# Turned scores from a second product instead of turned probabilities, division once per unit, and attention written in one hand order

## The chip, the cores and the metric

The kernel runs on one core of a Trainium2 chip. The metric is the device time of one execution in microseconds (us). "PE" is the matmul engine, with its weight loads shown apart as "PEld"; DVE, ACT and POOL are the vector, scalar and GpSimd engines; SP issues most of the DMAs.

## The reference

Input x has S = 2048 tokens of D = 1024; there are H = 32 heads of width 32, N = 4 segments of L = 512 tokens, and a channel MLP with F = 3584. All is float32.

```python
def _A_ref(x, wq, wk, wv, wo, beta):            # x is layernormed
    q, k, v = (x @ wq, x @ wk, x @ wv)          # split to [B, H, N, L, Dh]
    g = sigmoid(beta)
    for s in range(N):
        logits = einsum("bhqd,bhkd->bhqk", qs, ks) * Dh ** -0.5 + causal_mask
        a_dot = einsum("bhqk,bhkd->bhqd", softmax(logits), vs)
        pq = phi(qs)                            # phi(t) = t + 1 if t > 0 else exp(t)
        a_mem = einsum("bhld,bhde->bhle", pq, M) / (einsum("bhld,bhd->bhl", pq, z) + 1e-6)
        outs.append(g * a_mem + (1 - g) * a_dot)
        M = M + einsum("bhld,bhle->bhde", phi(ks), vs);  z = z + phi(ks).sum(l)
    return concat(outs) @ wo

h = x + _A_ref(layernorm(x), ...)
return h + gelu(layernorm(layernorm(h)) @ w1 + b1) @ w2 + b2
```

## The kernel before, in words

**Precision.** Every operand of a product is kept as two numbers of a shorter format, a high half (`hi`, names ending in h) and the rest (`lo`, names ending in l), and a product is three matmuls (`mm3`, lines L116 to L118): high by high, high by low, low by high. A high half is a cast on ACT or DVE, a low half a subtraction on DVE or POOL.

**Stages.** The tokens are processed in two halves of 1024, each half two segments. Per half: layernorm and turning of the tokens to [channels, tokens] (`ln1`), attention, the output projection (`wo_first`, `wo_second`), the second layernorms, and the MLP by a scheme of seven products (lines from L840 on). A unit of attention is one column group g (of 8, four heads of 32 each) and one segment: `dense` projects k, q and v in 24 steps of three 512-wide matmuls (tiles `kps`, `qps`, `vps`), and between those steps `heads` runs the four heads of the unit before.

**One head before.** `stack` copies high and low halves of q and k by DMA into 96-row tiles `qs` and `ks`, so that a single 96-row product is the sum of the three. `qk` (L543, L544) multiplies for each block i of 128 queries the queries (stationary) by all keys up to the diagonal, widths 128 to 512, into `pqk` (two banks); DVE adds the mask, scales by -1/sqrt(32), writes `pr` to SBUF and keeps the row's minimum in `mx`. `soft` (L552) takes the exponential on ACT with the row sums as a by-product. `ptr` (L593, L595) turns the ten 128x128 blocks of probabilities on PE, by a product with the identity, into `ppt` (two banks), ACT casts them to `pth`; `sub` (L600) gives the low half `ptl` on DVE. `av` (L613) multiplies by `vs`, which holds the high and low halves of v as 64 stationary columns, into the single bank `po`; ACT copies the lower 32 rows to `ot` (L618) and DVE adds the upper ones (L624). `inverse` and `weigh` make the reciprocals of the sums of a unit, bring them from a row per query to a column per query over `r_dram`, and multiply on POOL.

**Order before.** The order on each engine in the attention comes from the scheduler of the programming layer, out of the order in which the code records its instructions: generators are interleaved by ratios (`interleave`, RA, RH, RS), and the table `PLAN` says which operation of which head stands in each of the six steps of a slot. Only the opening and the MLP stand in `in_order`, which ties every instruction to the one recorded before it on its engine.

**Memory of the segments.** `smalls` interleaves small matmuls that read the memory (`pm`) and update it (`pmm`) between the others; `pkn`, `vn` and `pom` are turnings of 128x128 blocks. They all, the projections and `pwo` share three banks (tag "d").

## Time and profile before

| | |
|---|---|
| median of 3 runs | 2315.74 us (2314.35 to 2320.98) |
| span of the profiled execution | 2309.1 us |
| PE busy | 2273.1 us, 98% |
| PE weight loads | 1895.7 us, 82% |
| DVE busy | 1519.7 us, 66% |
| ACT busy | 1227.7 us, 53% |
| POOL busy | 830.6 us, 36% |
| instructions | 34959 |

The profiled execution's time outside its span is not recorded; the median of the runs lies 6.6 us above that span. Busy is the union of the instructions' durations; a matmul's duration contains its way through the array, which overlaps the next one, so the pace of PE is read from the starts in the timeline. In a row of groups, the two numbers after the count are the total busy time in us and the mean of one in ns, and behind the second bar stands the idle time of the engine just before these instructions and what ended it. Attention lies at about 38 to 555 us and 895 to 1435 us of the span.

### The profile page before, as it was taken

How to read it: one execution, taken by the hardware profiler on the slowest of the kernel's cores; microseconds unless marked ns; L12 is line 12 of the kernel's file. 1: busy time of each engine (PE TensorE's matmuls, PEld its weight loads, DVE VectorE, ACT ScalarE, POOL GpSimd, SP SyncE). 2: the span in 40 equal slices, each digit the busy share in tenths (PEclk: the TensorE clock that was granted, in tenths of full speed). 3: DMA queues.
4: the chain of work that ended last, by engine and by line, in shares of the span. 5: the costliest groups of instructions: out<-in, count | busy, mean ns of one | idle time of the engine just before them, and what ended most of it. 6: DMA issues, size and time to landing. Idle time of an engine off the chain costs nothing.

```text
span 2309.1 us, 34959 instructions
## 1 busy us (share of the span) xinstructions
PE 2273.1 (98%) x11801; PEld 1895.7 (82%) x11801; DVE 1519.7 (66%) x3045; ACT 1227.7 (53%) x2581; POOL 830.6 (36%) x686
## 2 busy tenths in 40 slices
PE   8999999999999999999999998999999999999999
PEld 6888888877888887888888886788888888888887
DVE  6777777776655565777777776574566766566663
ACT  6777777774453445777777775363344223332221
POOL 4222222224244442233232224244445654155430
PEclk9999999999999999999999999999999999999999
DMA  6333343344466654433333343466567976476772
GB/s 187 104 95 97 98 102 95 94 140 164 138 209 173 186 166 138 120 100 95 95 95 99 95 118 119 160 202 195 156 190 265 348 249 217 152 259 218 249 235 92
DMA packets 329885, 364.00 MB, mean 158 GB/s; under 512 B 28750, under 2 KB 221802, under 8 KB 329706
## 3 DMA queue, kind: packets, MB, share of 16 engines
q1 hardware_dynamic: 266538, 325.06, 46.5%
q10 hardware_dynamic: 63168, 36.71, 5.3%
q8 instruction: 93, 1.52, 0.3%
q14 instruction: 86, 0.70, 0.1%
HBM read 234.98 MB, written 76.35 MB: 135 GB/s over the span
## 4 chain that ended last, share of the span: by engine, by line
PE 69%; DMA 1%; POOL 1%; ACT 1%; DVE 1%; issue 1%; SPq 0%; POOLq 0%; ACTq 0%; DVEq 0%
PE po L1300 23%; PE bps L904 10%; PE cps L904 7%; PE dps L904 6%; PE po L613 3%; PE ppt L593 3%; PE pqk L543 2%; PE vps L116 1%; PE vps L117 1%; PE vps L118 1%; PE kps L116 1%; PE kps L117 1%; PE qps L117 1%; PE qps L116 1%; PE kps L118 1%; PE qps L118 1%
## 5 line engine op out<-in xcount | busy, mean ns | idle before, releaser
L552 ACT ACTIVATE pr<-pr,mx 128x256 f32<-128x256 f32 (+3 forms) x512 | 287.1, 561 | 163.5 <-DVE mx L544 154.7
L544 DVE CUSTOM_DVE_ANT_0 pr<-pqk,mask 128x256 f32<-128x256 f32 (+3 forms) x512 | 244.5, 486 | 107.1 <-PE pqk L543 105.9
L600 DVE TENSOR_TENSOR ptl<-ppt,pth 128x512 fp32r<-128x512 f32 (+1 forms) x384 | 227.3, 600 | 94.9 <-ACT pth L595 92.4
L593 PE MATMUL ppt<-ident,pr 128*128 128x128 f32 x1280 | 223.1, 277 | 1.0 <-DVE ptl L600 0.8
L595 ACT CAST pth<-ppt 128x512 fp32r<-128x512 f32 (+1 forms) x384 | 194.0, 517 | 40.2 <-PE ppt L593 33.1
L93 POOL TENSOR_TENSOR wl<-wr,wh 128x1024 fp32r<-128x1024 f32 x52 | 124.8, 2399 | 229.5 <-PE pqk L543 128.0
L1310 DVE TENSOR_TENSOR c<-c,po 128x512 f32<-128x512 f32 x160 | 105.4, 683 | 149.6 <-PE po L1300 146.7
L593 PEld LDWEIGHTS ppt<-ident,pr 128*128 128x128 f32 x1280 | 165.0, 141 | 30.8 <-DVE ptl L600 1.9
L543 PE MATMUL pqk<-ks,qs 96*128 96x256 f32 (+3 forms) x512 | 161.6, 316 | 0.0
L613 PE MATMUL po<-ptl,vs 128*64 128x512 f32 (+3 forms) x512 | 154.1, 310 | 4.3 <-DVE ptl L600 4.1
L613 PE MATMUL po<-pth,vs 128*64 128x512 f32 (+3 forms) x512 | 156.0, 327 | 0.0
L1300 PE MATMUL po<-w2h,zh 128*128 128x512 f32 x378 | 120.8, 389 | 0.0
L543 PEld LDWEIGHTS pqk<-ks,qs 96*128 96x128 f32 x512 | 96.5, 189 | 21.6 <-issue 0.2
L904 PE MATMUL bps<-zh,sb 128*128 128x512 f32 x336 | 111.1, 391 | 0.0
L904 PE MATMUL bps<-zh,sa 128*128 128x512 f32 x336 | 110.8, 390 | 0.0
L1157 POOL TENSOR_TENSOR w2r<-w2r 128x512 f32<-128x512 f32 x54 | 85.5, 1595 | 70.2 <-DMA w2r<-in_B_w 63.6
L116 PE MATMUL vps<-yh,wh 128*128 128x512 f32 x256 | 109.4, 427 | 0.9 <-DVE MZ L500 0.9
L116 PE MATMUL kps<-yh,wh 128*128 128x512 f32 (+1 forms) x264 | 110.0, 417 | 0.0
L116 PE MATMUL qps<-yh,wh 128*128 128x512 f32 x256 | 106.9, 418 | 0.0
L1300 PE MATMUL po<-w2h,hl 128*128 128x512 f32 x322 | 103.0, 390 | 0.0
L117 PE MATMUL kps<-yl,wh 128*128 128x512 f32 (+1 forms) x264 | 102.3, 388 | 0.1
L118 PE MATMUL kps<-yh,wl 128*128 128x512 f32 (+1 forms) x264 | 101.9, 386 | 0.0
(253 smaller groups left out, 6548.4 us busy)
## 6 DMA issues: line engine op xcount, KB each, us to landing
hr<-h_dram SPq DMA_DIRECT2D x112, 448.0 KB, 5.7
w2r<-in_B_w SPq DMA_DIRECT2D x122, 256.0 KB, 4.1
r<-in_B_w SPq DMA_DIRECT2D x56, 512.0 KB, 4.8
h_dram<-ht ACTq DMA_DIRECT2D x84, 256.0 KB, 3.8
ks<-kh SPq DMA_DIRECT2D x256, 64.0 KB, 2.0
qs<-qh SPq DMA_DIRECT2D x256, 64.0 KB, 2.0
wr<-in_A_wo SPq DMA_DIRECT2D x32, 512.0 KB, 4.5
wx<-in_B_w SPq DMA_DIRECT2D x56, 256.0 KB, 3.6
```

The lines of the kernel that those rows point to most:

```text
L116: nc.tensor.matmul(ps, ah, bh, start=first, stop=False)
L117: nc.tensor.matmul(ps, ah, bl, start=False, stop=False)
L118: acts["mm"] = nc.tensor.matmul(ps, al, bh, start=False, stop=last)
L543: nc.tensor.matmul(pqk[:, :n], u["qs"][j][:, i * P:(i + 1) * P], u["ks"][j][:, 0:n], start=True, stop=True)
L544: nc.vector.tensor_tensor_reduce(out=st["pr"][:, offs[i]:offs[i] + n], in0=pqk[:, :n], in1=mask[:, 512 - n:512], op0=ALU.add, op1=ALU.min, ...
L552: nc.scalar.activation(pi, pi, AF.Exp, bias=mx[:, i:i + 1], scale=-1.0, accum_out=mx[:, 4 + i:5 + i])
L593: nc.tensor.transpose(ppt[:, o:o + P], pr[:, offs[i] + jk * P:offs[i] + (jk + 1) * P], ident)
L595: acts["pth"] = n, nc.scalar.copy(pth[:, base:base + w], ppt[:, :w])
L600: nc.vector.tensor_tensor(o, x0, x1, op=ALU.subtract)
L613: nc.tensor.matmul(po[:, P * jk:], v, st[part][:, koff[jk]:koff[jk] + w], start=(jk, part) == (0, "pth"), stop=(jk, part) == (2, "ptl"))
L904: nc.tensor.matmul(ps, x_[:, c, :], y_[:, c, :], start=first and c == 0 and n == 0, stop=last and c == 3 and n == 2, skip_group_check=True)
L1300: nc.tensor.matmul(ps, x_[:, k], y_[k], start=opens and k == 0 and i == 0, stop=closes and k == self.KP - 1 and i == 2, skip_group_check=True)
```

## The change: what it does

The probabilities are no longer turned. `qk1` makes the score product as before, but for the maximum alone: DVE writes its result back over the bank. When a unit's four heads are through, `halves` splits the maxima (negative) into two halves, `turn` brings them with four 8-column products from queries in partitions to queries in columns (`ptn`), and `rows` copies them as eight more rows (96 to 103) into `qs`; the same rows of `ks` hold a pattern of ones that picks the two rows of a head. `qk2` then makes a second product with the keys stationary, 104 rows deep: its output `pst` is the turned score less the maximum. ACT takes the exponential into `e` (three groups of 512, 384 and 256 + 128 columns), POOL zeroes the upper triangle of the diagonal blocks with an affine select, ACT casts to `ph` (`cast`), DVE makes `pl` (`lows`). `vs` gets two columns of ones, so that the row 64 of `po` is the sum of the probabilities; ACT copies it to `sm`. Division comes once per unit (`weigh`): two DVE transposes of 32x32 blocks around one reciprocal and the gate, then multiplications on POOL by quarters. The trip over `r_dram` goes.

The units come in another order (`ORDER`): column groups 0 and 1 alternate in the first four units of a half and 6 and 7 in the last four, so weights are loaded and split in 12 sets per half where it was 8. Weights' high halves are made on DVE, the low halves on POOL in quarters. Attention and the first output projection stand in `in_order` on all engines, and every operation that isn't a dense matmul has a step by hand (`at`); a slot is six steps, one head passes `qk1` in slots h + 3 and h + 4, `qk2` in h + 8 and `av` in h + 9. The output weights of the first block are made within the last units, and the second projection takes over the weights that the first used last.

```diff
-PLAN = ('q1 r S2', 'q0 a0', 'q2 t0 w a1', 'q3 s0 o', 't1', 's1 t2')
+ORDER = [(g + n % 2, n // 2) for g in (0,) for n in range(4)] + [(n // 2, n % 2) for n in range(4, 12)] + \
+    [(6 + n % 2, n // 2) for n in range(4)]
+KX = 104
+QK = {4: 3, 5: 2, 1: 1, 2: 0}
+AVS = {2: (0,), 4: (1,), 5: (3, 2)}
+VC = 66
...
-            pqk = psum.tile([P, 512], F32, tag="qk", name="pqk", bufs=2)
-            nc.tensor.matmul(pqk[:, :n], u["qs"][j][:, i * P:(i + 1) * P], u["ks"][j][:, 0:n], start=True, stop=True)
-            nc.vector.tensor_tensor_reduce(
-                out=st["pr"][:, offs[i]:offs[i] + n], in0=pqk[:, :n], in1=mask[:, 512 - n:512],
-                op0=ALU.add, op1=ALU.min, scale=-SCALE, scalar=3.0e38, accum_out=st["mx"][:, i:i + 1])
-            soft(st, i)
...
+            ps = psum.tile([P, 512], F32, tag="qk", name="pqk", bufs=2)
+            nc.tensor.matmul(ps[:, :n], u["qs"][0:96, j, i * P:(i + 1) * P], u["ks"][0:96, j, 0:n], start=True, stop=True)
+            nc.vector.tensor_tensor_reduce(out=ps[:, :n], in0=ps[:, :n], in1=mask[:, 512 - n:512], op0=ALU.add,
+                                           op1=ALU.min, scale=-1.0, scalar=3.0e38, accum_out=u["mx"][:, i, j:j + 1])
+        def halves(u):
+            u["mh"] = mh = ab.tile([P, 4, 8], F32R, name="mh", bufs=2)
+            m3 = mh.rearrange("p i (j x) -> p i j x", x=2)
+            nc.vector.tensor_copy(m3[:, :, :, 0], u["mx"][:, :, 0:4])
+            nc.vector.tensor_tensor(m3[:, :, :, 1], u["mx"][:, :, 0:4], raw(m3[:, :, :, 0]), op=ALU.subtract)
+        def turn(u):
+            ps = u["pt"] = psum.tile([P, 512], F32, tag="pt", name="ptn", bufs=2)
+            for i in range(4):
+                nc.tensor.matmul(ps[0:8, i * P:(i + 1) * P], u["mh"][:, i, :], acts["identr"], start=True, stop=True)
+        def rows(u, j):
+            nc.scalar.copy(u["qs"][96:KX, j, :], u["pt"][0:8, :])
+        def qk2(h, n):
...
+            ps = psum.tile([P, 512], F32, tag="pt", name="pst", bufs=2)
...
+                nc.tensor.matmul(ps[:, o:o + 512 - P * jk], u["ks"][:, j, jk * P:(jk + 1) * P], u["qs"][:, j, jk * P:512],
+                                 start=True, stop=True)
+            e = e[:, :w]
+            nc.scalar.activation(e, ps[:, :w], AF.Exp, scale=SCALE)
...
+            nc.gpsimd.affine_select(d, d, pattern=[[0, 2], [1, P]] if n == 2 else [[1, P]], compare_op=ALU.is_ge,
+                                    fill=0.0, base=0, channel_multiplier=-1)
+        def cast(h, n):
+            e, ph, _ = H4[h][n]
+            nc.scalar.copy(ph, e)
+        def lows(h, n):
+            e, ph, pl = H4[h][n]
+            nc.vector.tensor_tensor(pl, e, raw(ph), op=ALU.subtract)
...
-                    nc.tensor.transpose(ppt[:, o:o + P], pr[:, offs[i] + jk * P:offs[i] + (jk + 1) * P], ident)
-            acts["pth"] = n, nc.scalar.copy(pth[:, base:base + w], ppt[:, :w])
...
+        def out(h):
+            nc.scalar.copy(u["ot"][b, :], po[32:64, :])
+            nc.scalar.copy(u["sm"][32 * j:32 * j + 1, :], po[64:65, :])
+        def weigh(u, k):
+            if k == 0:
+                nc.vector.transpose(smt, sm)
+            elif k == 1:
+                nc.vector.reciprocal(u["inv"], smt.rearrange("p (a b) -> p a b", b=32)[:, :, 0])
+                nc.gpsimd.tensor_scalar(u["inv"], u["inv"], gcol[:, u["g"]:u["g"] + 1], None, op0=ALU.mult)
+            elif k == 2:
+                nc.vector.transpose(sm.rearrange("p (a b) -> p a b", b=32),
+                                    u["inv"].unsqueeze(2).to_broadcast([P, 16, 32]))
...
+        def slot_step(t, c):
+            h1, h2, h3 = t - 4 + c // 4, t - 8, t - 9
...
+            if c in QK and ok(h1):
+                qk1(h1, QK[c])
+                if QK[c] == 0 and h1 % 4 == 3:
+                    u = U[h1 // 4]
+                    at(b + 4, partial(halves, u))
+                    at(b + 6, partial(turn, u))
+                    for j in range(4):
+                        at(b + 7 + j, partial(rows, u, j))
+            if c > 2 and ok(h2):
+                qk2(h2, c - 3)
+                at(b + c + 2, partial(cast, h2, c - 3))
+                at(b + c + 3 + (c == 5), partial(lows, h2, c - 3))
+            if c in AVS and ok(h3):
+                av(h3, AVS[c])
+                if c == 5:
+                    out(h3)
+                    at(b + 6, partial(added, h3))
...
+        order = ExitStack()
+        order.enter_context(in_order())
         rest = attention(half, first)
...
+        interleave(wo_first(half, hts), rest, RA, RH, RS)
+        order.close()
```

784 lines of the change are left out of this document (426 added, 358 removed).

## The prediction

> **What bounds the kernel now.** I read the busy shares first, then the windows of the attention stage, then its matmuls in order of time, and last the groups of the engines beside TensorE.
>
> ```profile
> PE 2273.1 (98%) x11801; PEld 1895.7 (82%) x11801; DVE 1519.7 (66%) x3045; ACT 1227.7 (53%) x2581; POOL 830.6 (36%) x686
> ```
>
> TensorE is busy for 98% of the span, but that is an average; the change touches the attention of both halves alone, so its stages decide. "Head" below is one head of one segment (128 in all, 64 per half); a unit is four heads of one column group.
>
> ```profile
> core 0 of [0], span 2309.1 us
> core 0: us, PE busy (x) PEld busy (x) DVE busy (x) ACT busy (x) POOL busy (x), PEclk, DMA share, GB/s
> 100.00:480.00 380.00, 379.32 (x2327) 322.33 (x2326) 276.65 (x785) 277.52 (x715) 97.05 (x103) 1.00 0.37 95
> 945.00:1340.00 395.00, 395.00 (x2427) 336.07 (x2426) 291.82 (x842) 292.92 (x751) 116.12 (x116) 1.00 0.37 96
> 500.00:560.00 60.00, 54.09 (x293) 43.95 (x292) 41.94 (x89) 37.51 (x81) 19.88 (x15) 0.97 0.40 137
> 1380.00:1450.00 70.00, 62.45 (x321) 50.29 (x320) 45.20 (x95) 38.30 (x80) 26.86 (x21) 0.98 0.43 141
> ```
>
> The two long windows are the steady part of each half: PE has no idle time in the second, while DVE has 26%, ACT 26% and POOL 71%. The clock is full. The two short windows are the ends of attention, where PE lost 5.9 us of 60 and 7.6 us of 70. So in the steady part PE sets the pace and whatever leaves it shortens the span, until the next engine takes over. The pace of one head follows from the score products:
>
> ```profile
> 945.00:1340.00 395.00, 64.35 (x205) 38.52 (x205) 97.44 (x205) 1.00 0.37 96
> ```
>
> There are four weight loads of `pqk` per head (PEld, x205), so 51.25 heads in 395 us: 7.71 us per head. DVE works 0.739 x 7.71 = 5.70 us of that (291.82 of 395 us), ACT 5.72 us.
>
> **The change part by part.** *The turning transposes go, a second score product comes.* A matmul's duration (0.39 us for 512 columns) overlaps the next, so PE work is priced from start to start:
>
> ```profile
> 303.42 0.39 PE L543 MATMUL pqk<-ks,qs 96*128 96x512 f32 x1
> 303.65 0.40 PE L116 MATMUL vps<-yh,wh 128*128 128x512 f32 x1
> 303.89 0.40 PE L117 MATMUL vps<-yl,wh 128*128 128x512 f32 x1
> 304.12 0.39 PE L118 MATMUL vps<-yh,wl 128*128 128x512 f32 x1
> 304.35 0.60 PE L593 MATMUL ppt<-ident,pr 128*128 128x128 f32 x4
> 304.71 0.48 PE L116 MATMUL vps<-yh,wh 128*128 128x512 f32 x1
> 305.03 0.40 PE L117 MATMUL vps<-yl,wh 128*128 128x512 f32 x1
> ...
> 305.93 0.38 PE L593 MATMUL ppt<-ident,pr 128*128 128x128 f32 x2
> 306.07 0.48 PE L116 MATMUL vps<-yh,wh 128*128 128x512 f32 x1
> 306.38 0.40 PE L117 MATMUL vps<-yl,wh 128*128 128x512 f32 x1
> 306.62 0.40 PE L118 MATMUL vps<-yh,wl 128*128 128x512 f32 x1
> 306.85 0.28 PE L543 MATMUL pqk<-ks,qs 96*128 96x256 f32 x1
> 306.97 0.39 PE L116 MATMUL vps<-yh,wh 128*128 128x512 f32 x1
> ```
>
> Four `ppt` transposes hold the next matmul back by 0.36 us (304.35 to 304.71), and the matmul behind them takes 0.32 us where such a one takes 0.23 (303.42 to 303.65): 0.45 us together. Two cost 0.14 + (0.31 - 0.23) = 0.22 us (305.93 to 306.38). A head has groups of 4, 4 and 2: 0.45 + 0.45 + 0.22 = 1.12 us. The second product `pst` has the widths of `pqk`: 512 columns take 0.23 us, 256 take 0.12 (306.85 to 306.97), 384 and 128 by their widths 0.17 and 0.06: 0.58 us. It contracts 104 rows where `pqk` contracts 96; `vps` with 128 rows and `pqk` with 96 both take 0.23 us for 512 columns, so I take the same. The weighted sums keep their widths and get 66 stationary columns where there were 64: nothing. Per unit four 128-column turns of the maxima come (4 x 0.06 = 0.24 us) and one `pw` transpose goes (about 0.16 us by the rows of two). Sum on PE: 128 x (0.58 - 1.12) + 32 x (0.24 - 0.16) = -69.1 + 2.6 = **-66.5 us**, which leaves 7.71 - 0.52 = 7.19 us per head. The PE order, in the middle of a projection's unit, before and after:
>
> ```order
> L116 MATMUL vps<-yh_9229,wh 128x512
> L117 MATMUL vps<-yl_9230,wh 128x512
> L118 MATMUL vps<-yh_9229,wl 128x512
> L543 MATMUL pqk<-ks,qs 128x384
> L593 MATMUL ppt<-ident,pr 128x128 x4
> L613 MATMUL po<-pth,vs 64x128
> L613 MATMUL po<-ptl,vs 64x128
> L613 MATMUL po<-pth,vs 64x256
> L613 MATMUL po<-ptl,vs 64x256
> ```
>
> ```order
> L124 MATMUL vps<-yh_10288,wh 128x512
> L125 MATMUL vps<-yl_10289,wh 128x512
> L126 MATMUL vps<-yh_10288,wl 128x512
> L595 MATMUL pqk<-ks_10244,qs_10246 128x384
> L624 MATMUL pst<-qs_10246,ks_10244 128x256
> L624 MATMUL pst<-qs_10246,ks_10244 128x128
> L654 MATMUL po<-ph,vs_10252 66x128
> L654 MATMUL po<-pl,vs_10252 66x128
> L654 MATMUL po<-ph,vs_10252 66x256
> L654 MATMUL po<-pl,vs_10252 66x256
> ```
>
> The transposes' place is taken by the second product; the rest of the step stands as it stood.
>
> The Trainium skill ("TensorE: Matmul & The Clock Gate", Part 4) puts a 128x128 transpose at about 275 ns inside a kernel; as a price for each of the 1280 that would be an estimated 352 us, and a time some 209 us below mine. The trace has the same figure as a duration (0.60 us for four that overlap), but four of them advance PE by 0.36 us, so the sum goes by the start times.
>
> *ACT stays level.*
>
> ```profile
> L552 ACT ACTIVATE pr<-pr,mx 128x256 f32<-128x256 f32 (+3 forms) x512 | 287.1, 561 | 163.5 <-DVE mx L544 154.7
> ```
>
> ```profile
> L595 ACT CAST pth<-ppt 128x512 fp32r<-128x512 f32 (+1 forms) x384 | 194.0, 517 | 40.2 <-PE ppt L593 33.1
> ```
>
> ```profile
> 306.37 0.59 ACT L458 CAST pkh<-pkn 128x512 fp32r<-128x512 f32 x1
> 306.85 0.61 ACT L366 ACTIVATE e<-qps 128x512 f32<-128x512 f32 x1
> 307.34 0.61 ACT L367 ACTIVATE r<-qps 128x512 f32<-128x512 f32 x1
> 307.81 0.39 ACT L595 CAST pth<-ppt 128x256 fp32r<-128x256 f32 x1
> 308.23 0.51 ACT L552 ACTIVATE pr<-pr,mx 128x256 f32<-128x256 f32 x1
> 308.64 0.19 ACT L552 ACTIVATION_READ_ACCUMULATOR pr<-pr,mx 128x1 f32 x1
> 308.77 0.62 ACT L448 CAST pqh<-pq 128x512 fp32r<-128x512 f32 x1
> ```
>
> Gone: 287.1 + 194.0 + 512 reads of 0.19 = 97, together 578 us. New, per head: three exponentials out of PSUM (512, 384, 384 columns; 0.59 + 0.49 + 0.49, between the 0.59 and 0.39 of the casts out of PSUM at 306.37 and 307.81), three casts from SBUF (0.62 + 0.52 + 0.52, by `pqh`), one more copy of the sums (0.59) and one of four turned rows (0.59): 4.41 us x 128 = 564 us. No loss, no gain: PE hides it.
>
> *DVE gets fuller.*
>
> ```profile
> L600 DVE TENSOR_TENSOR ptl<-ppt,pth x384: 393/692/694, 49.8 to 1431.9; 128x512 fp32r<-128x512 f32 x128, 128x256 fp32r<-128x256 f32 x64
> ```
>
> ```profile
> L90 DVE CAST wh<-wr 128x1024 fp32r<-128x1024 f32 x43 | 29.4, 684 | 0.2
> ```
>
> ```profile
> L559 DVE RECIPROCAL rs<-mx 128x4 f32<-128x4 f32 x128 | 22.4, 175 | 30.4 <-ACT pr L552 30.2
> ```
>
> The maximum keeps its four instructions, now written back to PSUM (same price taken; no row shows it). The low halves keep 1280 elements per head, so 1.8 us at 692 ns per 512. Per head a reciprocal goes (0.18). Per unit come two small splits of the maxima (0.17 each), a reciprocal and two 32x32 transposes of 128x512 (no row; 0.69 each like any 512-wide pass, bounds 0.3 and 1.4). Because the first and last four units alternate column groups, 24 weight sets are split where 16 were, and all on DVE: 80 casts for 44, 36 x 0.684 / 32 = 0.77 us per unit. Together 2.67 / 4 - 0.18 = +0.5: 6.2 us per head of 7.19.
>
> *POOL* is new in the path, zeroing the diagonal blocks between ACT's exponential and ACT's cast:
>
> ```profile
> L93 POOL TENSOR_TENSOR wl<-wr,wh 128x1024 fp32r<-128x1024 f32 x52 | 124.8, 2399 | 229.5 <-PE pqk L543 128.0 <-DVE wh L90 46.8 <-ACT wh L92 25.3
> ```
>
> ```profile
> L337 POOL TENSOR_SCALAR_AFFINE_SELECT mask<-mask 128x128 f32<-128x128 f32 x2 | 0.6, 297 | 0.1
> ```
>
> Two selects of 128 and one of 256 columns: 0.30 + 0.30 + 0.4 = 1.0 us per head; weight lows (2.4 us x 3 x 24 sets) 1.35, weighing and `pql` (0.6 us per 256 columns by the same row) about 0.9, smaller ones some 0.4: some 3.7 us of 7.19. It fits, and two steps of slack stand between each select and its cast.
>
> *Waits of the hand order.* All engines now run strictly as written. Two loops are short. First, the turned maxima sit in one of two `pt` banks until ACT has copied four rows, the last behind an exponential, and the next score product waits for that bank. ACT, in the middle of a half, in a plain step before and at the unit's turn now (`ph` casts the probabilities `e`, `qs<-ptn` is a copied row):
>
> ```order
> L595 CAST pth<-ppt 128x512
> L552 ACTIVATE pr,mx<-pr,mx 128x384
> L618 COPY ot<-po 32x512
> L552 ACTIVATE pr,mx<-pr,mx 128x512
> L595 CAST pth<-ppt 128x512
> ```
>
> ```order
> L637 CAST ph<-e 128x384
> L611 CAST qs_181<-ptn 8x512 x2
> L627 ACTIVATE e<-pst 128x512
> L611 CAST qs_181<-ptn 8x512
> L627 ACTIVATE e<-pst 128x384
> ```
>
> The exponentials now read `pst`, and the last row copy stands between two of them. Long ACT instructions in a row start 0.48 us apart (306.37, 306.85, 307.34 above). From the start of the first `pst`: 0.39 for the matmul, 0.48 and 0.58 on ACT, some 0.1 for signals = 1.55; PE itself needs 0.23 + 3 x 0.23 + 0.23 = 1.15 before it wants the bank. Wait 0.4 us per unit: +13 us (0 if ACT's queue is short, 0.4 per head = 51 at worst). Second, the weighted sums have one bank, `po`. Behind its last matmul lie an exponential, ACT's copy and DVE's add: 0.3 + 0.48 + 0.58 + 0.68 = 2.0; PE has nine projection matmuls and two small ones until it wants the bank, 9 x 0.23 + 0.12 + 0.06 = 2.25. DVE, around the add of one head's sums (`ot`, now `side`), before and now:
>
> ```order
> L544 ISA pr,mx<-pqk,mask 128x512
> L544 ISA mx 128x1
> L624 TENSOR_TENSOR ot<-po,ot 32x512
> L431 TENSOR_TENSOR ql<-qps,qh 128x512
> L559 RECIPROCAL rs<-mx 128x4
> ```
>
> ```order
> L596 ISA pqk,mx<-pqk,mask 128x384
> L596 ISA mx 128x1
> L382 SCALAR_TENSOR_TENSOR pq<-e,r 128x512
> L641 TENSOR_TENSOR pl<-e,ph 128x512
> L670 TENSOR_TENSOR side<-po,side 32x512
> ```
>
> The add stood right behind a maximum; a low half is now always ahead of it, and in some slots one more pass of 0.69 us, which eats the 0.25 of slack. I take 0.1 us per head on average: +13 us (bounds 0 and 0.4).
>
> *Ends.* The output weights of the first projection are now split inside the order, and the second reuses what the first left, so these waits should go:
>
> ```profile
> PE pwo L117 <- POOL zl L93: 3.1, 1, 3.1
> ```
>
> ```profile
> PE pwo L117 <- POOL zl L93: 4.7, 1, 4.7
> ```
>
> -8 us (bounds 0 and -12). Against it the second unit now needs a new weight set within 10 dense steps of 0.7 us, 7 us for a load, a cast and four lows: +5 us (0 to 10).
>
> Sum: 2309.1 - 66.5 + 13 + 13 - 8 + 5 = 2265.6 us of span; the median of the runs lies 6.6 us above this span (2315.74 - 2309.1), so **2272 us**. With no new wait and the ends at their best it is 2309.1 - 66.5 - 12 + 6.6 = 2237; with the waits nearly doubled 2295.
>
> **The rivals.** *The short loops eat the gain.* PE waits 0.4 us in every head, not 0.2. With no gain at the ends that is 2309.1 - 66.5 + 51 + 5 + 6.6 = 2305 us. For it: strict order, one `po` bank. Against: the loops' slack is positive in plain slots.
>
> *DVE becomes the bound (slower).* The low halves used to read PSUM and SBUF; now both inputs, `e` and `ph`, lie in SBUF, while POOL works half the time. A row of the later stage shows what that does:
>
> ```profile
> L1032 DVE TENSOR_TENSOR sa<-s,sa 128x512 fp32r<-128x512 f32 x56 | 52.5, 974 | 32.4 <-ACT sa L1031 32.4
> ```
>
> `sa`, whose two inputs lie in SBUF while POOL adds, has a mean of 974 ns; `ptl`, of the same width with one input in PSUM, never exceeds 694. At that mean each low half costs 0.28 more: 6.2 + 3 x 0.28 = 7.05 us of DVE per head. If strict order leaves DVE idle for 12% of its time, a head takes 7.9 us, +0.2 over now: 2315.7 + 26 = 2342. It decides once DVE's work and waits pass 7.71 us. Against: the new POOL instructions are 0.3 to 0.65 us long where those of the later stage are whole tiles of 512 columns, 1.2 us by the same 2.4 per 1024, so each hold is shorter. The Trainium skill ("SBUF — State Buffer", Who interferes with whom) says that a VectorE instruction with two SBUF inputs contends with a GpSimd one that reads SBUF; by that rule, with which `sa` and `ptl` agree, this rival is the one to fear.
>
> *The transposes were not on the path*, so nothing moves: 2316. Against it stands the PE window with no idle time.
>
> **How the numbers follow.** My forecast has 0.57 (its own range 2237 to 2295), the loops 0.18, DVE 0.21, no effect 0.04. About 0.3% (7 us) is what a measurement of this kernel can tell. The forecast is all faster; of the loops' 0.18 about 0.12 lie below 2309; of the last two about 0.01 do. Faster 0.70 (0.57 + 0.12 + 0.01). Same 0.08: 0.04 of the loops and no effect. Slower 0.22: 0.02 of the loops, 0.20 of DVE. The range runs from 2237 to 2338: it holds the forecast, the loops, no effect and the better half of the DVE case.
>
> **What would show it.** Right: PE rows of `pst` at the pace of `pqk`; about 7.4 us per head; short PE waits at `pst` for ACT and at `po` for DVE; `pl` with a mean under 800 ns; DVE below 90% in the steady windows. Wrong: `pl` means near 1 us with PE waiting on DVE throughout (the DVE rival), PE waits above 0.4 us in each head (the loops), or a pace still at 7.7 with PE full.

## The result: slower by 1.7%, and the profile after

The changed kernel takes 2355.3 us (median of 4 runs, 2353.1 to 2359.9) against 2316.2 before (2314.4 to 2321.0): ratio 1.0174, 95% interval 1.0153 to 1.0194. The forecast was 2272, with a range up to 2338, so the result lies outside it on the slow side. The profiled execution has a span of 2352.8 us, 43.7 more than before.

The busy times of the page, and the groups that answer to the rows of the prediction (behind the second bar stands the idle time just before a group and what ended it):

```profile
PE 2255.7 (96%) x11129; PEld 1849.4 (79%) x11129; DVE 1605.5 (68%) x3094; ACT 1238.6 (53%) x2153; POOL 1150.4 (49%) x1445
L641 DVE TENSOR_TENSOR pl<-e,ph 128x384 fp32r<-128x384 f32 (+1 forms) x384 | 262.5, 685 | 28.9 <-ACT ph L637 26.9
L654 PE MATMUL po<-ph,vs 128*66 128x512 f32 (+3 forms) x512 | 150.2, 319 | 46.5 <-DVE side L670 46.5
L624 PE MATMUL pst<-qs,ks 104*128 104x512 f32 (+3 forms) x512 | 141.1, 317 | 9.7 <-ACT e L627 8.8
L670 DVE TENSOR_TENSOR side<-po,side 32x512 f32<-32x512 f32 x128 | 87.0, 680 | 49.1 <-ACT side L664 25.8 <-ACT sm L664 22.1
```

PE's busy time fell, by 17 us, and its idle time rose from 36 to 97 us. Half of that idle time, 46.5 us, stands ahead of the first product of a head into `po`, and what ended it is DVE's add (`side`, L670).

The lines of single tiles give the stages (first and last start in us; before, then after): the projections end with the last `vps`, the last head with the last `po`, the output projections with the last `pwo`.

```profile
L118 PE MATMUL vps<-yh,wl x128: 389/393/400, 30.4 to 500.3; 128*128 128x512 f32 x128
L613 PE MATMUL po<-ptl,vs x256: 220/333/522, 53.0 to 552.9; 128*64 128x512 f32 x64, 128*64 128x128 f32 x64
L118 PE MATMUL pwo<-wh,ol x64: 388/389/628, 501.3 to 620.0; 128*128 128x512 f32 x64
```

```profile
L126 PE MATMUL vps<-yh,wl x128: 388/392/628, 29.0 to 506.9; 128*128 128x512 f32 x128
L654 PE MATMUL po<-pl,vs x256: 221/333/592, 78.6 to 578.1; 128*66 128x512 f32 x64, 128*66 128x128 f32 x64
L126 PE MATMUL pwo<-zh,ol x32: 389/392/397, 605.3 to 641.0; 128*128 128x512 f32 x32
```

In the first half the projections end 6.6 us later (506.9 for 500.3), and the output projection takes 134.1 us where it took 119.7. The last head passes `po` 71 us behind the last projection; before it was 53. The second half repeats this: by the same rows its projections are 3 us longer (487.7 for 484.7) and its output projection 14 us (135.2 for 121.5). The first MLP stage and the last one add 1 and 5 us. So two thirds of the added time lie in the output projections.

In the steady part nothing was gained. The rows of the score products (in brackets the counts: matmuls, weight loads and reductions of `pqk`, four to a head each), 120 to 460 us, before and after:

```profile
120.00:460.00 340.00, 55.39 (x176) 33.08 (x176) 83.86 (x176) 1.00 0.38 96
```

```profile
120.00:460.00 340.00, 55.69 (x176) 32.89 (x175) 84.38 (x176) 1.00 0.37 96
```

Both kernels pass 44 heads in these 340 us, 7.7 us a head; the forecast was about 7.4.

**PE's losses by its starts.** A matmul's duration hides short gaps, so below PE's time is split by its starts. From each start to the next goes PE's own pace, read from undisturbed pairs: 0.2315 us for 512 columns, 0.174 for 384, 0.117 for 256, 0.06 for 128, 0.109 from one turned block of 128x128 to the next and 0.028 from the last of them to what follows. The matmul right behind turned blocks takes 0.08 us more; that is counted with PE's own work too. The rest is a loss, charged to the later instruction. In some stretches of 3.4 or 6.8 us the profile's granted clock is 0.5, and there 512 columns take 0.427 us; this extra stands in a row of its own. Over both projections and both output projections:

| us | before | after |
|---|---|---|
| PE's own work | 1163.3 | 1101.3 |
| of it the transposes `ppt`, with the pause behind them | 140.7 | gone |
| of it the second product `pst` | | 74.6 |
| loss at `po` | 8.1 | 70.2 |
| loss at `pst` | | 15.7 |
| loss at `kps`, `qps`, `vps` (projections) | 6.7 | 21.2 |
| loss at `pqk` | 0.1 | 10.1 |
| half clock | 2.8 | 7.1 |
| other losses | 29.8 | 22.7 |

So PE got 62 us lighter, and its losses grew by 99.5. The sum is the 37.5 us that these stretches are longer (1210.8 before, 1248.3 after). (The expectations further below were written with a rougher split of the same starts, in which a part of the transposes' cost counts as loss: it has 9.5 us per half at `po` before and 31 after, where this one has 4 and 35.) One such wait, in a slice of the timeline after (start, us, engine, line):

```profile
1135.76 0.28 PE L654 MATMUL po<-pl,vs 128*66 128x256 f32 x1
1135.96 0.48 ACT L627 ACTIVATE e<-pst 128x384 f32<-128x384 f32 x1
1136.47 0.58 ACT L663 COPY side<-po 32x512 f32<-32x512 f32 x1
1137.06 0.58 ACT L664 COPY sm<-po 1x512 f32<-1x512 f32 x1
1137.35 0.42 DVE L492 TENSOR_TENSOR om<-pm,rg 128x256 f32<-128x256 f32 x1
1137.69 0.98 DVE L641 TENSOR_TENSOR pl<-e,ph 128x512 fp32r<-128x512 f32 x1
1138.20 0.22 PE L595 MATMUL pqk<-ks,qs 96*128 96x128 f32 x1
1138.60 0.67 DVE L670 TENSOR_TENSOR side<-po,side 32x512 f32<-32x512 f32 x1
1139.42 0.41 PE L654 MATMUL po<-ph,vs 128*66 128x512 f32 x1 [0.99 <-DVE side L670]
```

Between a head's last product into `po` and the next head's first stand an exponential, two copies on ACT, a low half and the add on DVE: 3.66 us here. PE had run out of other work at 1138.26, so it lost 1.16. Most heads lose less; the mean is 0.45 us in the projections (49.0 us over the 109 heads that pass there).

The longest stretch at half clock in the projections, from 937.2 to 944.0 us (granted clock 0.51, third figure from the end of the first row), begins at the end of a stop of 2.9 us, in which PE waits for a DMA at the start of the second half:

```profile
937.20:944.00 6.80, 6.21 (x18) 5.21 (x19) 2.42 (x7) 1.91 (x3) 5.58 (x11) 0.51 0.45 102
937.79 0.77 PE L595 MATMUL pqk<-ks,qs 96*128 96x512 f32 x1 [2.91 <-DMA qs<-side]
938.35 0.63 PE L124 MATMUL vps<-yh,wh 128*128 128x512 f32 x1
938.78 0.63 PE L125 MATMUL vps<-yl,wh 128*128 128x512 f32 x1
```

If such a stop brings the half clock, which no run tests by itself, a wait costs more than its own length.

The chain of waits, from 1080 to 1200 us, before and after, by line:

```profile
by line: PE po L613 15.2%; PE ppt L593 15.0%; PE pqk L543 7.7%; PE vps L117 6.3%; PE vps L116 6.2%; PE qps L117 6.2%; PE qps L116 6.2%; PE qps L118 6.1%; PE vps L118 6.1%; PE kps L116 5.8%; PE kps L117 5.8%; PE kps L118 5.6%; PE pm L398 2.4
```

```profile
by line: PE po L654 12.9%; issue 12.4%; PE pst L624 6.8%; PE vps L124 6.2%; PE vps L126 6.2%; PE vps L125 6.2%; PE pqk L595 5.5%; PE qps L124 3.6%; PE kps L124 3.5%; PE qps L125 3.3%; PE qps L126 3.2%; PE kps L125 3.1%; PE kps L126 3.1%; AC
```

Before, the whole chain of these 120 us lies on PE: the order that the scheduler found kept PE fed. After, PE has 70% of it, "issue" 12%, ACT 11%, DVE 5.5% and POOL 1%.

### The profile page after: what moved, and what is told of

Same layout as the page of the kernel before. It is cut to its first block, busy times and chain, and to the rows that moved or that the text cites. A ratio compares the mean times of both kernels' runs of the same rounds, so it can differ in the third digit from the quotient of the medians.

```text
span 2352.8 us, 33994 instructions
## 1 busy us (share of the span) xinstructions
PE 2255.7 (96%) x11129; PEld 1849.4 (79%) x11129; DVE 1605.5 (68%) x3094; ACT 1238.6 (53%) x2153; POOL 1150.4 (49%) x1445
## 4 chain that ended last, share of the span: by engine, by line
PE 43%; DMA 4%; issue 4%; ACT 3%; DVE 3%; POOL 3%; SPq 0%; ACTq 0%; POOLq 0%; DVEq 0%
PE po L1465 17%; PE bps L1069 4%; PE cps L1069 3%; PE dps L1069 3%; PE po L654 2%; DMA s_dram<-hr 1%; PE pst L624 1%; PE pqk L595 1%; DMA hr<-h_dram 1%; PE vps L124 1%; PE pwo L125 1%; PE pwo L126 1%; PE pwo L124 1%; PE vps L126 1%; PE vps L125 1%
## 5 line engine op out<-in xcount | busy, mean ns | idle before, releaser
L596 DVE CUSTOM_DVE_ANT_0 pqk<-pqk,mask 128x512 f32<-128x512 f32 (+3 forms) x512 | 246.0, 496 | 84.2 <-PE pqk L595 81.6
L641 DVE TENSOR_TENSOR pl<-e,ph 128x384 fp32r<-128x384 f32 (+1 forms) x384 | 262.5, 685 | 28.9 <-ACT ph L637 26.9
L627 ACT ACTIVATE e<-pst 128x384 f32<-128x384 f32 (+1 forms) x384 | 200.4, 530 | 99.7 <-PE pst L624 93.3
L746 POOL TENSOR_TENSOR wl<-wr,wh 128x256 fp32r<-128x256 f32 x264 | 222.8, 853 | 48.7 <-issue 25.1
L631 POOL TENSOR_SCALAR_AFFINE_SELECT e<-e 128x128 f32<-128x128 f32 (+1 forms) x384 | 151.4, 397 | 193.9 <-ACT e L627 189.6
L637 ACT CAST ph<-e 128x384 fp32r<-128x384 f32 (+1 forms) x384 | 209.6, 549 | 44.5 <-POOL e L631 41.3
L654 PE MATMUL po<-ph,vs 128*66 128x512 f32 (+3 forms) x512 | 150.2, 319 | 46.5 <-DVE side L670 46.5
L595 PE MATMUL pqk<-ks,qs 96*128 96x512 f32 (+3 forms) x512 | 162.7, 318 | 7.8 <-DMA qs<-side 2.9
L654 PE MATMUL po<-pl,vs 128*66 128x512 f32 (+3 forms) x512 | 156.6, 311 | 2.5 <-DVE pl L641 2.4
L624 PE MATMUL pst<-qs,ks 104*128 104x512 f32 (+3 forms) x512 | 141.1, 317 | 9.7 <-ACT e L627 8.8
L654 PEld LDWEIGHTS po<-ph,vs 128*66 128x66 f32 x512 | 68.6, 138 | 74.6 <-DVE side L670 51.7
L670 DVE TENSOR_TENSOR side<-po,side 32x512 f32<-32x512 f32 x128 | 87.0, 680 | 49.1 <-ACT side L664 25.8
```

Of the source, the lines that this page charges most:

```text
L595: nc.tensor.matmul(ps[:, :n], u["qs"][0:96, j, i * P:(i + 1) * P], u["ks"][0:96, j, 0:n], start=True, stop=True)
L596: nc.vector.tensor_tensor_reduce(out=ps[:, :n], in0=ps[:, :n], in1=mask[:, 512 - n:512], op0=ALU.add, op1=ALU.min, scale=-1.0, scalar=3.0e ...
L624: nc.tensor.matmul(ps[:, o:o + 512 - P * jk], u["ks"][:, j, jk * P:(jk + 1) * P], u["qs"][:, j, jk * P:512], start=True, stop=True)
L627: nc.scalar.activation(e, ps[:, :w], AF.Exp, scale=SCALE)
L631: nc.gpsimd.affine_select(d, d, pattern=[[0, 2], [1, P]] if n == 2 else [[1, P]], compare_op=ALU.is_ge, fill=0.0, base=0, channel_multipli ...
L637: nc.scalar.copy(ph, e)
```

## The experiments

Own work and losses are PE's, by starts, over both projections; "tails" is the time of both output projections. Ratios are to the kernel before, which took between 2313 and 2316 us in the different sets of runs; differences of a few us between two kernels of different sets say little.

| kernel | ratio (95%) | own work | loss | of it at `po` | of it half clock | tails |
|---|---|---|---|---|---|---|
| before | 1 | 944.1 | 25.5 | 4.7 | 0.0 | 241.1 |
| after | 1.0174 (1.0153 to 1.0194) | 876.0 | 103.0 | 49.0 | 4.0 | 269.3 |
| e1 add first | 1.0446 (1.0430 to 1.0461) | 876.0 | 157.8 | 86.6 | 7.1 | 281.2 |
| e2 no bank add | 1.0245 (1.0219 to 1.0271) | 876.1 | 114.4 | 24.0 | 4.2 | 274.4 |
| e3 no select | 1.0138 (1.0123 to 1.0153) | 876.0 | 98.7 | 44.7 | 3.0 | 266.6 |
| e4 slower tail | 1.0133 (1.0115 to 1.0152) | 876.0 | 99.7 | 47.9 | 4.0 | 264.8 |
| e5 narrow maximum | 1.0163 (1.0145 to 1.0180) | 876.0 | 99.5 | 46.2 | 4.3 | 271.0 |
| e6 weights on ACT | 1.0253 (1.0235 to 1.0271) | 876.0 | 123.6 | 48.3 | 4.8 | 270.8 |
| e7 no order | 1.1167 (1.1150 to 1.1184) | 876.0 | 327.2 | 162.0 | 59.7 | 274.2 |
| e8 PE ordered only | 1.1228 (1.1211 to 1.1246) | 876.0 | 322.5 | 164.8 | 50.2 | 292.1 |
| e9 sums aside | 1.0177 (1.0160 to 1.0194) | 876.0 | 105.3 | 46.8 | 8.1 | 272.4 |
| e10 e2 and e5 | 1.0231 (1.0202 to 1.0260) | 876.0 | 114.2 | 26.7 | 6.9 | 275.6 |
| e11 block maximum | 1.0147 (1.0132 to 1.0162) | 834.6 | 138.1 | 61.0 | 9.2 | 273.5 |
| e12 and two `po` banks | 1.0133 (1.0118 to 1.0148) | 834.6 | 131.4 | 17.8 | 9.3 | 274.4 |
| e13 e5, low halves on DVE | 1.0222 (1.0203 to 1.0240) | 876.0 | 108.0 | 50.3 | 8.6 | 270.2 |
| e14 e12, low halves on DVE | 1.0061 (1.0043 to 1.0079) | 834.6 | 117.1 | 26.7 | 4.6 | 271.7 |
| e15 and slower tail | 1.0045 (1.0029 to 1.0061) | 834.6 | 118.9 | 26.6 | 6.5 | 268.0 |
| e16 and scores later | 1.0041 (1.0028 to 1.0054) | 834.4 | 115.5 | 22.4 | 5.2 | 268.8 |
| e17 and two banks in the tail | 1.0029 (1.0020 to 1.0039) | 834.4 | 116.7 | 21.3 | 5.8 | 264.1 |
| e18 POOL not ordered | 1.0378 (1.0363 to 1.0394) | 876.0 | 154.2 | 60.8 | 22.2 | 269.8 |

**One wait or load at a time.** The first theory (A) was that the closed loop at `po` costs the time.

```diff
-                    at(b + 6, partial(added, h3))
+                    todo.setdefault(b + 6, []).insert(0, partial(added, h3))
```

> Change: DVE's add of a head's upper rows of po (side) stands ahead of the first low half (pl, 512 wide) of its step, not behind it; nothing else moves. Theory A (the single po bank: the bank is free only when DVE's add has run, and PE stands at the next po for it; by the starts in PE's timeline PE loses 31 us at po in each half after the change and 9.5 before): the add starts about one pl, 0.7 us, sooner in every head, the loss at po falls from 31 to 10 to 16 us per half, and the time from 2355 to 2315 to 2330. Theory B (DVE is the pace maker, because the low halves contend with POOL in SBUF and strict order leaves it no more room): DVE's work is the same, so the wait only moves to another PE instruction: 2350 to 2360.

Measured 2418.4 us, 63 more than the changed kernel. DVE now stands at the add and waits for ACT's copies, 168.9 us in all where it was 49.1, and the low halves behind it are late for PE:

```profile
L670 DVE TENSOR_TENSOR side<-po,side 32x512 f32<-32x512 f32 x128 | 87.0, 679 | 168.9 <-ACT side L664 88.3 <-ACT sm L664 79.2 <-PE vps L126 1.5
L654 PE MATMUL po<-pl,vs 128*66 128x512 f32 (+3 forms) x512 | 164.0, 325 | 38.6 <-DVE pl L641 37.6
```

An add that is ready too late for its place costs more than a place too far back: in a strict order everything behind it waits too.

```diff
-            po = H4.pop(h)["po"]
+            H4.pop(h)
-            nc.vector.tensor_tensor(u["ot"][b, :], po[0:32, :], u["ot"][b, :], op=ALU.add)
+            nc.vector.tensor_tensor(u["ot"][b, :], u["ot"][b, :], u["ot"][b, :], op=ALU.add)
```

> Leaves out part of the computation: the rows 0 to 31 of po (one half of the values' product) are not added; DVE's add keeps its place, width and count but reads only SBUF. So the po bank waits for ACT's two copies alone. Theory A: the loss of PE at po falls from 31 us per half to 10 or less; time 2355 - 2 x 21 = 2313, at most 2325. Theory B: DVE has the same work in the same order, and the time stays within 2345 to 2360.

Measured 2370.3 us. The loss at `po` in the projections did fall, from 49 to 24 us, as A said, and the time rose by 15 us. The waits came back at other places (at `vps` 24 us for 6, at `pst` 17 for 6), and the add itself got longer when both its inputs lay in SBUF, 845 ns for 680:

```profile
L670 DVE TENSOR_TENSOR side<-side 32x512 f32<-32x512 f32 x128 | 108.1, 845 | 13.8 <-ACT side L663 10.2
L624 PE MATMUL pst<-qs,ks 104*128 104x512 f32 (+3 forms) x512 | 142.0, 319 | 22.9 <-ACT e L627 22.2 <-ACT qs L611 0.6
```

So the loop at `po` holds PE, but shortening it did not shorten the time. The longer add (0.165 us a head, 21 us of DVE in all) clouds this run; e12 below opens the loop without it, and A alone falls there too.

```diff
-            nc.gpsimd.affine_select(d, d, pattern=[[0, 2], [1, P]] if n == 2 else [[1, P]], ...)
```

> Leaves out part of the computation: POOL's affine selects on the diagonal blocks of e (the upper triangle is not zeroed). POOL loses 384 instructions, 151 us of its 1150. Theory B (contention of DVE's low halves with POOL): the mean of pl falls from 685 to about 600 ns (0.26 us per head) and the time by 25 to 35 us, to 2320 to 2330. Theory A: pl is 0.05 to 0.1 us shorter ahead of each add, which gives back that much per head only: 2340 to 2350.

Measured 2347.4 us, 8 below the changed kernel, what A's line said (2340 to 2350). The mean of `pl` stayed: 690 ns, for 685. The selects are not what makes the low halves long.

```profile
L639 DVE TENSOR_TENSOR pl<-e,ph 128x384 fp32r<-128x384 f32 (+1 forms) x384 | 264.6, 690 | 25.0 <-ACT ph L635 23.4
```

```diff
-RA, RH, RS = 1.3, 64, 1.3
+RA, RH, RS = 1.3, 16, 0.95
```

> Change: behind the last projection the remaining 66 steps of the heads are spread over nearly all 64 products of the first output projection (0.95 steps per product from the 16th on, where it was 1.3 throughout), so that a head there has 6.3 output products beside it instead of 4.6; in the steady part it has 6 projection products. Theory C (the tail is too dense: nine heads are left where about four were left before, and PE loses 10.5 us at po and 4.7 at pst there in each half): both losses fall to a third, 10 us per half, 2355 to 2335. If the heads only finish later and the second output projection waits for them: 2350 to 2365. Theory B says nothing of it: DVE is busy 67% there.

Measured 2347.2 us, between the two lines of the expectation. The loss at `pst` in the tails fell from 9.7 to 2.8 us, that at `po` from 21.2 to 16.6; the tails are 4.5 us shorter and still 24 longer than before.

```diff
-            nc.vector.tensor_tensor_reduce(out=ps[:, :n], in0=ps[:, :n], in1=mask[:, 512 - n:512], ...)
+            nc.vector.tensor_tensor_reduce(out=ps[:, n - P:n], in0=ps[:, n - P:n], in1=mask[:, 384:512], ...)
```

> The maximum is taken over the 128 columns of the diagonal block alone (four reduces of 128 columns per head instead of 128, 256, 384 and 512); the score product on PE, and every instruction's place, stay. The shift under the exponential is then another number of the same row. DVE loses about 0.9 us of its 6.3 per head in the steady part, nothing else changes. The bank add test (e2) took the wait at po away and the time did not fall, so theory A alone is out. Theory D (DVE in strict order is too full: 82% busy where the tail of each step waits for the next engine; any wait taken away at one place comes back at another): PE's waits in the projections (54 and 51 us by starts) fall to 25 or less each and the time from 2355 to 2290 to 2310. Theory A' (the latency of the chain PE, ACT, POOL, ACT, DVE under strict order, not DVE's fill): little moves, 2340 to 2355.

Measured 2349.3 us; the interval overlaps that of the changed kernel. In the same stretch, after and here, DVE's busy time (79.67 and 73.83 in the rows) fell from 80 to 74%, over six such stretches (160 to 460 and 1060 to 1360 us) from 80 to 72%:

```profile
1060.00:1160.00 100.00, 97.08 (x546) 79.92 (x545) 79.67 (x213) 76.33 (x148) 54.51 (x98) 1.00 0.36 91
```

```profile
1060.00:1160.00 100.00, 98.20 (x552) 80.70 (x551) 73.83 (x217) 76.33 (x147) 55.35 (x95) 1.00 0.34 86
```

That a fuller DVE bounds the changed kernel (theories B and D, and the third rival of the prediction) is refuted for DVE by itself: a tenth of its time set free buys at most a few us.

```diff
-        def wsplit(g, name, hi_eng="vector", step=None):
+        def wsplit(g, name, hi_eng="scalar", step=None):
```

> The high halves of the projection weights are cast on ACT instead of DVE, at the same steps (3 x 12 casts of 128x1024 per half, 0.68 us each on DVE, so 0.38 us less of DVE per head, about 1 us each on ACT). Theory D: 0.38 of the 0.9 of the narrow maximum, so some 40% of its gain: 2325 to 2340, if ACT's casts, 1 us in a queue that is 75% busy, don't hold up the exponentials. Theory A' (latency): ACT stands in every chain, so this costs: 2355 to 2375.

Measured 2371.9 us, in the range of theory A'. The loss at `pst` in the projections rose from 6 to 25 us. ACT has no room for a cast of 1 us (mean 1051 ns) in its place of the order, though it is busy for about 80% there.

**The order itself.**

```diff
-        order.enter_context(in_order())
         rest = attention(half, first)
```

> The hand order is taken off attention and the first output projection on all engines (the scheduler of the layer places the instructions, from the same recorded order); all instructions stay. If the strict order with a full DVE is the cause (D), a scheduler that lets DVE pass a waiting add or low half gives back a part: 2300 to 2340. If the scheduler finds the same order or puts dense work behind waits: 2345 to 2400.

```diff
-        order.enter_context(in_order())
+        order.enter_context(in_order(mybir.EngineType.PE))
```

> The hand order holds for PE alone in attention and the first output projection; DVE, ACT, POOL and SP are placed by the scheduler. D: as without any order, 2300 to 2340, and if PE's order is the good part of the hand order, below e7. If the order of the other engines doesn't matter: 2350 to 2360.

```diff
-        order.enter_context(in_order())
+        order.enter_context(in_order(*(e for e in mybir.EngineType if e != mybir.EngineType.Pool)))
```

> The changed kernel with the hand order on every engine but POOL, whose instructions the scheduler places. e8 (only PE bound) lost 240 us. Theory H, with POOL one of several queues that hold the groups up: if the scheduler puts the selects ahead of the weights' low halves, 2340 to 2355; if it puts them behind, 2360 to 2400; POOL's place is then a cost of the order either way.

Measured 2583.1, 2597.6 and 2401.4 us: all slower, the first two outside both of their expectations, the third at the edge of its second one. Without it on DVE the loss at `po` is more than three times as large (162 and 165 us for 49): PE stands up to 7.3 us for the add (the waits of PE in e8: us in all, times, longest):

```profile
PE po L654 <- DVE side L670: 176.5, 98, 7.3
```

Some 70 us of each of the first two times are half clock (69 and 67 us with the tails, for 7 in the changed kernel). So the hand order is no loss by itself; this recording needs it, on POOL too.

**Two and three at a time.**

```diff
-            nc.scalar.copy(u["sm"][32 * j:32 * j + 1, :], po[64:65, :])
+            nc.scalar.copy(u["sm"][32 * j:32 * j + 1, :], u["ot"][32 * j:32 * j + 1, :])
```

> Leaves out part of the computation: ACT's second copy at a head's end, the row of the sums, is read from the row that the first copy has written in SBUF, not from the bank po. Its place, width and count stay. In e1 DVE's add never began before this second copy had ended (copies from 1104.36 to 1105.53, add at 1105.56); in e2, where the add does not read po, it began with the end of the first. Theory F (the loop behind the last po product: ACT's exponential, two copies of 0.58 us and DVE's add of 0.68, about 2.6 us with signals, against the 2.25 us of work that PE has until it wants the bank): the add may start 0.58 us sooner, PE's loss at po falls from 21 us per half to 8 to 14, the time from 2355 to 2330 to 2345, not further, since e2 showed that other waits follow. If DVE's queue alone decides when the add runs: 2350 to 2358.

Measured 2354.7 us: no change, and the loss at `po` fell by 2 us only. But the edit did not open the loop. The second copy now reads a row of `ot` that DVE's add overwrites, and the add still never began before the second copy had ended (within 0.1 us behind it in 83 of 128 heads, in the changed kernel in 79). DVE's waits for L664, the second copy, stayed:

```profile
L670 DVE TENSOR_TENSOR side<-po,side 32x512 f32<-32x512 f32 x128 | 87.0, 680 | 55.1 <-ACT side L664 29.1 <-ACT sm L664 23.6 <-PE kps L125 1.0
```

So this run tests neither theory F nor its rival.

> e2 and e5 together: leaves out the addition of po's rows 0 to 31 (DVE's add reads only SBUF), and the maximum is taken over the diagonal block alone. Each of the two by itself took away a wait (e2: 25 us of PE's losses at po over both projections) or a load (e5: 9 points of DVE's 81%) and did not shorten the projections by more than 4 us. Theory G (two limits of almost the same height, the loop at po and DVE's queue; taking one away shows the other): together they shorten each projection by 10 to 20 us: 2355 to 2315 to 2335. If a third limit (ACT's queue in the chain of the exponentials) holds the pace: 2345 to 2365.

(Both edits as in e2 and e5.) Measured 2370.1 us, as e2, whose longer add it shares (860 ns). Theory G in its simple form, two limits, finds no support.

```diff
-            nc.tensor.matmul(ps[:, :n], u["qs"][0:96, j, i * P:(i + 1) * P], u["ks"][0:96, j, 0:n], ...)
-            nc.vector.tensor_tensor_reduce(out=ps[:, :n], ...)
+            nc.tensor.matmul(ps[:, c], u["qs"][0:96, j, c], u["ks"][0:96, j, c], start=True, stop=True)
+            if i == 0:
+                nc.vector.tensor_reduce(u["mx"][:, :, j], ps.rearrange("p (a b) -> p a b", a=4),
+                                        axis=mybir.AxisListType.X, op=ALU.max, negate=True)
```

> The first score product is made for the four diagonal blocks alone (4 x 128 columns per head instead of 1280, all in one bank), and the maximum is one reduce over the four blocks, without the mask. The shift under the exponential is the maximum of the row's diagonal block; result otherwise as before. PE loses 768 columns per head, 0.35 us at the pace of 0.23 per 512, 44 us in all; DVE loses four reduces with their read-outs (2.5 us) against one pass of 512 (0.7): -1.8 us per head. Theory F/G: two thirds of PE's 0.35 lie outside the stretch between a head's last po product and the next head's first, so they come through, and the rest of the loop stays: 2305 to 2325. If a chain that doesn't hold PE's work sets the pace (ACT): 2340 to 2355.

```diff
-                st["po"] = psum.tile([P, 512], F32, tag="av", name="po", bufs=1)
+                tag, bufs = ("qk", 2) if h % 2 and h < 54 else ("av", 1)
+                st["po"] = psum.tile([P, 512], F32, tag=tag, name="po", bufs=bufs)
```

> As e11, and every second head's weighted sums go to one of the two banks that the scores no longer fill (tag qk; up to the last projection), so the loop at po is open there. Theory F/G: PE's loss at po in the projections, about 21 us per half, falls below 6, 25 to 30 us below e11: 2275 to 2300, below the kernel before. If ACT or DVE sets the pace: as e11 within 5 us.

Measured 2347.4 and 2344.6 us. This is the clearest pair: PE's own work in the projections fell by 41 us, and its losses rose by 35 (e11: 103 to 138). With two `po` banks the loss at `po` falls from 61 to 18 us, and 36 of these 43 us come back elsewhere: 13 at `pst`, and 12 at `pqk`, whose two banks the second `po` shares. Neither PE, nor DVE (68% busy in the six steady stretches of e12), nor the one bank sets the pace by itself. In the chain of waits of e12, from 1080 to 1200 us, POOL now has 13%, with the low halves of the weights and the selects behind them:

```profile
by line: issue 14.1%; PE po L657 10.4%; PE pst L626 7.2%; PE kps L124 6.2%; PE kps L126 5.5%; PE kps L125 5.4%; POOL wl L749 5.0%; PE vps L124 3.6%; PE qps L124 3.5%; PE vps L125 3.5%; POOL e L633 3.5%; PE vps L126 3.5%; ACT e L629 3.2%; PO
```

```diff
-                nc.gpsimd.tensor_tensor(l[:, c], wr[:, c], raw(h)[:, c], op=ALU.subtract)
+                nc.vector.tensor_tensor(l[:, c], wr[:, c], raw(h)[:, c], op=ALU.subtract)
```

(Quarters on POOL become halves on DVE; e13 adds this to e5, e14 to e12, and e15 is e14 with the numbers of e4.)

> From the changed kernel: the narrow maximum of e5 (DVE 0.9 us per head lighter), and the low halves of the projection weights go from POOL (four quarters of 0.85 us per weight, 36 weights per half) to DVE (two of 512 columns, about 0.7 us). DVE has then about what it had (81%), POOL 1.9 us less per head. Theory H (under strict order the pace is the longest chain through whichever queues hold up the groups of a head; in e12 the chain of waits runs for a large part over POOL's weight lows ahead of the selects): time 2349 (e5) to 2325 to 2340. If POOL doesn't hold anything in this kernel, in which the po loop is closed: 2340 to 2360.

> From e12 (diagonal-block maximum, two po banks): the low halves of the projection weights on DVE, as in e13. DVE 68 to 78%, POOL 56 to about 30%. Theory H: with the loop at po open, PE 0.35 us per head lighter, DVE with room and POOL light, nothing but ACT (77%) is left to hold the pace: projections 485 and 481 to 455 to 468, time 2345 to 2295 to 2315. If ACT's queue (strict order, 77% busy) holds the pace of all these kernels: 2335 to 2350.

> e14 with the slower interleaving of e4 behind the last projection. e4 by itself took 8 us off the changed kernel. 8 us below e14, if the losses at po and pst behind the last projection are the same there; 0 if they follow from POOL's queue and are gone in e14.

Measured 2363.4, 2327.5 and 2324.5 us. The same edit, POOL's low halves to DVE, costs 14 us with the `po` loop closed and DVE as full as it was (e13 against e5), and gains 17 with the loop open and DVE with room (e14 against e12). In e14 POOL is gone from the chain of the same stretch:

```profile
by line: PE po L657 14.2%; PE pst L626 9.4%; PE vps L124 6.6%; PE vps L126 6.2%; PE vps L125 6.2%; PE qps L124 5.8%; PE qps L125 5.0%; PE qps L126 5.0%; PE kps L124 4.9%; DMA ks<-kk 4.5%; PE kps L126 4.3%; PE kps L125 4.3%; PE pqk L596 3.3%
```

The slower tail takes off 3 us where 8 were expected, and the intervals overlap.

```diff
-QK = {4: 3, 5: 2, 1: 1, 2: 0}
+QK = {5: 3, 0: 2, 1: 1, 2: 0}
```

> From e15: the four diagonal-block products of a head's scores stand in steps 5, 0, 1, 2 instead of 4, 5, 1, 2, so the bank of the scores has three steps, not two, between DVE's reduce and the next head's first product (PE waited there 0.94 us once per unit in e14, for DVE's reduce, 0.8 us of it plain idle time). If these waits go and nothing takes their place: 0.9 x 32 = 29 us, 2324 to 2297; by what the earlier runs showed (a wait taken away comes back in part at the next place) 2305 to 2320.

```diff
-            if now[0] < 24 * 16:
-                return ps_dense(name)
-            return psum.tile([P, 512], F32, tag="qk", name=name, bufs=2)
+            return ps_dense(name)
-                tag, bufs = ("qk", 2) if h % 2 and h < 54 else ("av", 1)
+                tag, bufs = ("qk", 2) if h % 2 else ("av", 1)
```

> e16, and the two po banks also behind the last projection (the memory's small products go to the banks of the projections there). PE's losses at po behind the last projection are 8.6 and 10.6 us in e15; with two banks 3 each: 10 us below e16, if the small products don't hold up the output products: 2295 to 2310, which would be below the kernel before.

Measured 2323.0 and 2319.6 us, above both expected ranges. The loss at `pqk` in the projections went (16 to 1 us) and `pst` took its place (19 to 31 us). With everything together the new scheme comes to 0.3% above the kernel before, with 110 us less of PE's own work in the projections than that kernel has. The half clock costs e17 13.8 us with the tails, the kernel before 2.8; this difference is larger than the 6 us that are left between the two. No version beat the kernel before. The longest waits that the profile of e17 shows for PE in attention (us in all, times, longest):

```profile
PE pst L624 <- ACT e L627: 22.7, 30, 1.6
PE po L655 <- DVE pl L641: 16.4, 17, 2.3
```

## Why the prediction was wrong, by its steps

- **PE's work (-66.5 us): right.** The starts give -62.0. The transposes cost 1.10 us per head with the pause behind them (forecast 1.12), the second product 0.58 (forecast 0.58).
- **The waits of the hand order (+26 us): the step that failed.** All losses together grew by 99.5 us. At `po` the forecast had 0.1 us per head, +13 us; it was 0.49 (70.2 less 8.1, by 128 heads). The working made the loop behind a head's last product 2.0 us long and had 2.25 us of other work for PE, and called 0.25 us of slack enough. Measured from the start of the last product to the end of the add, the loop has a median of 2.94 us in the steady part: there are two copies of 0.58 us on ACT where one was counted, a low half and often `om` stand ahead of the add, and the sum of durations leaves out the waiting in the queues. The profile before could have warned: with a single copy the same loop had a median of 2.65 us there, harmless because 5.06 us went by until the next head's first product. But a better sum for this loop would not have given the time either: e2 and e12 shorten it or open it, and the time moves by +15 and, against e11, by -3 us.
- **The first loop (`pst`, +13 us):** +15.7 measured, but the agreement is luck. In the projections, where the turned maxima were to cause it, it is 6.1. The other 9.7 lie in the tails, and most of that is one wait in each of them (3.75 and 3.76 us) that has nothing to do with the maxima: POOL's multiplications of `weigh` stand between low halves of the output weights, ACT's cast of their result waits 5.2 us for them, and the next exponential stands behind that cast.

```profile
562.20 0.72 POOL L688 TENSOR_TENSOR side<-side,omt 128x256 f32<-128x256 f32 x1
562.96 0.62 ACT L100 CAST oh<-side 128x512 fp32r<-128x512 f32 x1 [5.22 <-POOL side L688]
564.25 0.45 PE L624 MATMUL pst<-qs,ks 104*128 104x256 f32 x2 [3.75 <-ACT e L627]
```

- **Ends (-8): wrong sign, +28.** The waits at `pwo` for POOL's `zl` (7.8 us) went as forecast, and 4.0 us of new ones came there for the output weights. What was not seen is that the new pipeline leaves more heads behind the last projection: 76 `po` products there per half where it was 48, at eight a head. PE's own work in the tails grew by 6 us, as it fell in the projections, and its losses there by 22, of which 18 at `po`; these stand in the losses of the points above as well. The +5 us for the second unit's weights did not show: PE's waits name no weight of the projections.
- **DVE at 6.2 us per head: right** (80% of 7.7 us). **ACT level and POOL "fits": true by the busy times, false as a reading.** ACT is at 74 to 77% and POOL at 42 to 68% in the steady stretches, and yet both hold the groups of a head up (e6, e14). Busy shares do not say whether an engine fits when every queue is strict.
- **The rivals.** The first (the loops eat the gain, 2305) named the mechanism, and its sign came: waits above 0.4 us in each head. Its 51 us stand against 62 at `po`; what it left out are the other losses and the tails. The third (DVE the bound, 2342) came nearest to the number, by chance: as the cause it is refuted by e5 and e11, and its sign, a `pl` mean near 1 us, did not come. The mean is 685 ns, under the 800 that the forecast allowed. Split by shape:

```profile
L641 DVE TENSOR_TENSOR pl<-e,ph 128x384 fp32r<-128x384 f32 x256 | 158.4, 621 | 3.9 <-ACT ph L637 2.3
L641 DVE TENSOR_TENSOR pl<-e,ph 128x512 fp32r<-128x512 f32 x128 | 104.1, 813 | 25.0 <-ACT ph L637 24.5
```

With no POOL instruction beside them the two shapes take 551 and 682 ns in the mean (103 of 256 and 19 of 128 of them), so by this split POOL's company costs some 0.27 us per head, not the 0.84 of this rival.

What the runs show is this: before, the chain of waits ran over PE alone, so PE's work was the time. The new scheme makes a head's groups pass PE, ACT, POOL, ACT, DVE and PE again, through short buffers (two `pt` banks, one `po`, `pl` and `ph` single for two of the three groups), with every queue in strict order. The waits that this brings refill PE's saving: 62 us lighter and 99.5 us more lost, at the old pace of 7.7 us per head and with longer ends. That several loops of nearly the same length hold the pace is the reading that fits all runs, but no run shows each loop by itself. With one or two waits or loads taken away the time moved by 0 to 11 us, or got worse by up to 17; with three at once (e14: DVE light, `po` open, POOL light) it fell by 28 us, and that with 41 us less of PE's own work. e11 shows most directly that a PE saving is refilled: 41 us of it gave 8. Which loop is the longest in e14 to e17, and whether it is ACT's queue, stays open: no run made ACT lighter. The 5 us in the last MLP stage, whose code is the same, are not explained.

## What to carry to other kernels

Work taken off the bounding engine is worth its time only while that engine stays the whole chain of waits; when the same edit sends each item through more engines and short buffers, sum up every loop from buffer release to next use, instruction by instruction, with all that stands ahead in each queue, and hold the sum against the same loop in the trace you have. When an added wait is removed and the time stays, do not look for the one culprit: remove two or three at once before judging any of them. Count as well how many items a deeper pipeline leaves for the end, and what is left there to hide them.
